# Two of three slices' denominators summed on DVE from a PSUM bank, softmax pieces on POOL, first block first

## The chip, the cores and the metric

The kernel runs on one core of a Trainium2 chip. The core has five engines that run side by side and meet at semaphores: TensorE (PE, matrix products), VectorE (DVE), ScalarE (ACT), GpSimd (POOL) and SyncE (SP, which here issues transfers). The working memory is SBUF. PE writes its results to PSUM, eight banks of 512 float32 columns on 128 partitions; DVE and ACT reach PSUM, POOL has no operand there. The metric is the device time of one execution in microseconds, lower is better. Before the change it is 1321.46 us, the median of three runs (1316.26, 1321.46 and 1323.95).

## The reference

Three layers follow each other on 8192 tokens of width D = 192.

```
w   = softmax(weight_gen)                 # per token: 8 heads x 7 taps
out[s, head] = sum_k w[s, head, k] * x[s - 6 + k, head's 24 columns]

h = out @ w_in                            # 192 -> 2048
g = (a0 + a1 h + a2 h^2 + a3 h^3) / (1 + |b0||h| + |b1| h^2 + 1e-6)
x = g @ w_out                             # 2048 -> 192

h = x @ w2_in                             # 192 -> 2048
y = (h * clip(h + 3, 0, 6) / 6) @ w2_out  # 2048 -> 192
```

The four weight matrices arrive as 64-bit floats, which the kernel takes apart into float32 on the chip.

## The kernel before

**Blocks and slices.** The tokens are cut into 17 blocks (`BL`): two of 256 tokens and fifteen of 512. The hidden width 2048 of a block is worked in slices of 512 PSUM columns: 8 slices for a small block (two groups of 128 hidden units beside each other), 16 for a large one, 256 slices in all. A product is split into high and low parts, so `in1`, `out1` (first layer) and `in2` (second layer) are each five matmuls per group of 128 hidden units. `out2` is done in float32, 32 matmuls of 192 columns for every 256 tokens. A pair of 128 tokens (index `u`) is transposed on PE (`xT`) after the convolution.

**The convolution.** A chunk of four tokens per partition (`c`) is loaded by `load_gen` and `load_chunk`; DVE does the softmax in `softmax_a` (maximum, subtraction) and `softmax_b` (sum, reciprocal, multiplication), ACT the exponential between them. `conv_mul` multiplies, on POOL nearly always, and `conv_sum` adds the seven taps on DVE.

**The rational function.** For a slice the numerator is made by `act_l`, `dve_t`, `dve_t2` and the quotient by `act_ln`, `act_exp`, `dve_hi` (high part), `pool_m`, `dve_d`, `pool_lo` (low part). The denominator has two forms. The usual one is `act_u` (|h|), `act_w` (|b1||h| + |b0|), `pool_q` (their product, on POOL), and later `act_q`. In a slice for which `whole(sl)` holds it is `act_v` (|b0 h|, written to SBUF, line 301), `act_s` (|b1| h^2, line 306) and `dve_q`, one `scalar_tensor_tensor` on DVE that adds both and 1 (line 311, both tensor inputs in SBUF). Here `whole` holds for every third of the first 96 slices (`QN`, `QK`, `QS`), 32 slices.

**What sets the order.** `plan()` is a list scheduler that runs before the program is built. Every step is entered with an engine, an assumed cost, a due time (from the constants `T`, `C1`, `XTP`, ...), what it follows and what it takes. At each turn it emits the step that can start first. It fixes one order per engine; on the chip each engine works through its own order and waits where an operand is late. Of PSUM's eight banks two hold `y1` (the first layer's output, one buffer); the other six go to two classes: `h` (first layer's hidden slices, `NH` = 4 at most) and `s` (`xT`, `in2`, `out2`, weight decoding; `NS` at most). At the end of a block `y1` is read out by a chain of five steps on ACT and DVE, `mid_y` to `tail_lo` (line 252); only then can `out1` of the next block start.

**Fill.** Where the plan leaves PE idle before the second layer of block 1, `idle_mm` (line 392) puts products of the identity matrix into the order.

Of the kernel before, what the change touches and what calls it, by code (L numbers as in the profile page):

```python
# [19 lines left out]
def kernel(  # L20
# [115 lines left out]
    def softmax_b(c):  # L136
        g = ex.pop(c)
        sg = two.tile([P, CT * H], F32, tag="mx", name="sg")
        nc.vector.tensor_reduce(out=sg, in_=g, axis=AX.X, op=ALU.add)
        nc.vector.reciprocal(out=sg, in_=sg)  # L140
        w = two.tile([P, K, CT * H], F32, tag="wk", name="wk")
        nc.vector.tensor_tensor(
            out=w.rearrange("p k t -> p t k"),
            in0=g[:, :, :K],
            in1=sg[:, :, None].to_broadcast([P, CT * H, K]),
            op=ALU.mult,
        )
# [5 lines left out]
    NS = 2  # L153
# [145 lines left out]
    def act_v(sl):  # L299
        u = two.tile([P, GW], F32, tag="u", name="u", bufs=NB["u"])  # L300
# [169 lines left out]
    def job_load(j):  # L470
        if moe_w_in.dtype == F32:
            if "w" not in j:
                j["w"] = two.tile(j["shape"], F32, tag="big", name="wf", bufs=ST)
# [10 lines left out]
        load_rows(sv, j["src"])  # L484
# [114 lines left out]
    JPU = 2.426
    PEN = 1.789  # L600
    CP = 2.57
    KP = 0.04
    WIN = 39.62
# [5 lines left out]
    XQ = -4.798
    XTP = 2.356  # L610
    XH = -5.949
    O1 = 4.624
    UM = 1.409
    I2 = -0.923
    SPR = 0.905
    R2 = -0.798
    O2 = 4.117
    OS = 0.714
    EV = 9.672
# [45 lines left out]
    for u, (b, v) in enumerate(UB):  # L665
        t0 = S0[b] * T - (BV[b] - 1 - v) * 8 * T
        c = u // 2
        if u % 2 == 0:
            t = t0 - CV * T
            add("gen", "SP", 0.6, t - XQ * T if c else X0P, load_gen, c, lat=2.0,  # L670
                take=[("wg", 2, [("softmax_b", c)])])
            add("load", "SP", 3.7, t - XQ * T + 1.0 if c else X0P + 0.5, load_chunk, c, lat=2.0,
                take=[("x", 2, [("conv_mul", 2 * c + 1, 1, 1)])])
# [4 lines left out]
        for i in range(2):
            for z in range(2):
# [256 lines left out]
```

## Time and profile before

| | before |
|---|---|
| median of the runs | 1321.46 us |
| the profiled execution | 1323.68 us, of which the span 1321.9 us |
| PE busy | 1293.3 us (98%), 6690 matmuls |
| DVE, ACT, POOL busy | 1117.8, 1134.5, 1149.9 us (85, 86, 87%) |
| mean granted PE clock | 0.992 of full |

The profiled execution is the one that all durations below come from. An engine's orders are in its own time: a long operation on DVE holds up everything that stands behind it in DVE's order. Matmul records overlap (a new one starts before the last has ended), so what a matmul takes from PE is read from one start to the next. A float32 matmul leaves two records; the fill products and `out2` are float32.

### The profile page before, as it was taken

What the parts mean: (1) busy time and instruction counts of PE and PEld (TensorE: products, weight loads), DVE (VectorE), ACT (ScalarE), POOL (GpSimd) and SP (SyncE); (2) the same over time, 40 slices, a digit from 0 to 9 for tenths busy, and PEclk for the clock granted to TensorE, in tenths of its full rate; (3) what the DMA queues carried; (4) which work ended last, traced back from release to release, by engine and by line L of the source; (5) the groups of instructions that cost most, each with busy time, mean ns of one, the idle gap of its engine ahead of it and who ended that gap; (6) DMA issues with size and microseconds to landing.
All of it is one profiled execution on the core that took longest, in us unless ns stands there. A gap on an engine that the chain in (4) does not pass through costs nothing.

```text
span 1321.9 us, 19246 instructions
## 1 busy us (share of the span) xinstructions
PE 1293.3 (98%) x6690; PEld 1136.3 (86%) x6690; DVE 1117.8 (85%) x1664; ACT 1134.5 (86%) x2032; POOL 1149.9 (87%) x921
## 2 busy tenths in 40 slices
PE   9789998999999999999999999999999999999998
PEld 9788886888988889898888889888888988888898
DVE  7989998999999898888899797988979788786841
ACT  6899898889898798989989798998989899897941
POOL 7898998898989889998999999898999989887830
PEclk9989998999999999999999999999999999999999
DMA  7431010101010101001010101001010000000000
GB/s 234 133 120 35 7 35 6 34 13 34 7 44 7 36 4 46 1 7 36 11 40 0 46 1 36 11 7 36 1 42 1 7 7 7 7 1 12 1 13 12
DMA packets 16121, 37.66 MB, mean 28 GB/s; under 512 B 1948, under 2 KB 12314, under 8 KB 16024
## 3 DMA queue, kind: packets, MB, share of 16 engines
q1 hardware_dynamic: 16024, 36.44, 8.5%
q8 instruction: 52, 0.85, 0.3%
q14 instruction: 45, 0.37, 0.1%
HBM read 30.14 MB, written 6.29 MB: 28 GB/s over the span
## 4 chain that ended last, share of the span: by engine, by line
PE 32%; ACT 21%; POOL 20%; DVE 17%; issue 7%; DMA 1%; SPq 0%; POOLq 0%; ACTq 0%; DVEq 0%
PE h L269 15%; PE y L444 10%; POOL w L368 6%; POOL w L331 6%; POOL glo L379 5%; ACT r L346 3%; ACT l L324 3%; DVE ghi L360 3%; ACT w L355 3%; ACT r L351 3%; DVE l L335 3%; POOL prod L167 3%; DVE w L372 2%; ACT w L317 2%; ACT g L427 2%
## 5 line engine op out<-in xcount | busy, mean ns | idle before, releaser
L379 POOL TENSOR_TENSOR glo<-w,r 128x512 fp32r<-128x512 f32 x256 | 334.0, 1306 | 40.6 <-DVE w L372 31.8
L368 POOL TENSOR_TENSOR w<-w,ghi 128x512 f32<-128x512 f32 x256 | 339.0, 1325 | 29.1 <-DVE ghi L360 22.0
L444 PE MATMUL y<-wo,g 128*128 128x192 f32 x2048 | 352.2, 326 | 0.0
L444 PEld LDWEIGHTS y<-wo,g 128*128 128x128 f32 x2048 | 338.6, 190 | 9.7 <-DVE w L372 0.4
L331 POOL TENSOR_TENSOR w<-w,u 128x512 f32<-128x512 f32 x224 | 291.3, 1303 | 26.9 <-ACT w L317 17.5
L372 DVE SCALAR_TENSOR_TENSOR w<-h,acol,w 128x512 f32<-128x512 f32 x256 | 190.8, 746 | 63.5 <-POOL w L368 62.4
L346 ACT ACTIVATE r<-w 128x512 f32<-128x512 f32 x256 | 162.5, 635 | 70.9 <-POOL w L331 57.3
L167 POOL TENSOR_TENSOR prod<-x,wk 128x672 f32<-128x672 f32 x127 | 192.2, 1525 | 16.4 <-DVE xc L182 10.0
L269 PE MATMUL h<-xh,wst 128*128 128x512 f32 (+1 forms) x544 | 206.0, 379 | 0.0
L269 PE MATMUL h<-xl,wst 128*128 128x512 f32 (+1 forms) x544 | 205.7, 378 | 0.0
L324 ACT ACTIVATE l<-h,acol 128x512 f32<-128x512 f32 x256 | 200.4, 783 | 4.3 <-DVE h L339 3.6
L335 DVE TENSOR_TENSOR l<-h,l 128x512 f32<-128x512 f32 x256 | 174.3, 684 | 35.0 <-ACT l L324 32.9
L360 DVE SCALAR_TENSOR_TENSOR ghi<-h,acol,r 128x512 fp32r<-128x512 f32 x256 | 190.1, 743 | 12.4 <-ACT r L351 11.9
L431 DVE SCALAR_TENSOR_TENSOR g<-g,h 128x512 f32<-128x512 f32 x256 | 174.1, 680 | 29.2 <-ACT g L427 28.5
L317 ACT ACTIVATE w<-u,bab 128x512 f32<-128x512 f32 x224 | 183.5, 819 | 14.7 <-POOL glo L379 14.0
L339 DVE SCALAR_TENSOR_TENSOR h<-l,acol,h 128x512 f32<-128x512 f32 x256 | 191.2, 750 | 4.5 <-ACT u L296 1.0
L427 ACT ACTIVATE g<-h 128x512 f32<-128x512 f32 x256 | 153.9, 601 | 13.8 <-PE h L269 13.7
L351 ACT ACTIVATE r<-r 128x512 f32<-128x512 f32 x256 | 161.6, 632 | 2.7
L355 ACT ACTIVATE w<-w 128x512 f32<-128x512 f32 x224 | 140.4, 627 | 0.0
L296 ACT ACTIVATE u<-h 128x512 f32<-128x512 f32 x224 | 132.8, 593 | 2.0 <-PE h L269 2.0
L408 PE MATMUL y<-ghi,wo1h 128*128 128x512 f32 (+1 forms) x272 | 114.3, 420 | 7.1 <-DVE xl L252 7.0
L269 PEld LDWEIGHTS h<-xl,wst 128*128 128x128 f32 x544 | 103.0, 189 | 19.3
(80 smaller groups left out, 2390.9 us busy)
## 6 DMA issues: line engine op xcount, KB each, us to landing
x<-in_x_dram SPq DMA_DIRECT2D x14, 960.0 KB, 4.7
st<-in_moe_w_out_dram SPq DMA_DIRECT2D x16, 384.0 KB, 3.2
out_dram<-osb SPq DMA_DIRECT2D x32, 192.0 KB, 1.8
st<-in_moe_w_in_dram SPq DMA_DIRECT2D x8, 512.0 KB, 4.9
st<-in_moe_w_in_dram SPq DMA_DIRECT2D x8, 256.0 KB, 4.4
wg<-in_weight_gen_dram SPq DMA_DIRECT2D x16, 112.0 KB, 2.9
x<-in_x_dram SPq DMA_DIRECT2D x1, 768.0 KB, 12.0
x<-in_x_dram SPq DMA_DIRECT2D x2, 216.0 KB, 4.8
```

The lines of the kernel that those rows point to most:

```text
L167: eng.tensor_tensor(out=pr.rearrange("p (h g) k -> p k h g", g=G), in0=xch[c][:, t : t + K, hs].rearrange("p k (h g) -> p k h g", g=G), in ...
L269: nc.tensor.matmul(out=dst, lhsT=l[:, fs], rhs=r, start=(n == 0), stop=(n == len(seq) - 1), skip_group_check=True,)
L317: nc.scalar.activation(out=w, in_=e1[sl]["u"], func=AF.Identity, scale=bab[:, 1:2], bias=bab[:, 0:1])
L324: nc.scalar.activation(out=l, in_=h1[sl], func=AF.Identity, scale=acol[:, 3:4], bias=acol[:, 2:3])
L331: nc.gpsimd.tensor_tensor(out=e["w"], in0=e["w"], in1=e["u"], op=ALU.mult)
L335: nc.vector.tensor_tensor(out=e["l"], in0=h, in1=e["l"], op=ALU.mult)
L346: nc.scalar.activation(out=r, in_=e["w"], func=AF.Ln, bias=0.0 if whole(sl) else CEPS)
L360: nc.vector.scalar_tensor_tensor(out=ghi, in0=h, scalar=acol[:, 0:1], in1=e["r"], op0=ALU.add, op1=ALU.mult)
L368: nc.gpsimd.tensor_tensor(out=m, in0=m, in1=g1[sl][0].bitcast(F32), op=ALU.mult)
L372: nc.vector.scalar_tensor_tensor(out=m, in0=h1.pop(sl), scalar=acol[:, 0:1], in1=m, op0=ALU.add, op1=ALU.subtract)
L379: nc.gpsimd.tensor_tensor(out=glo, in0=e["m"], in1=e["r"], op=ALU.mult)
L444: nc.tensor.matmul(out=y2[b, v][:, s, :], lhsT=g2[b, q][:, c : c + P], rhs=wo2[:, n, :], start=(n == 0 and s == 0), stop=(n == NF - 1), sk ...
```

## The change

The sum of the denominator reads |b0 h| from a PSUM bank, which `act_v` now writes; the bank is of class `s`, whose limit goes from 2 to 3. `whole` holds for two of every three slices, over the whole run: 171 instead of 32. The subtraction and the multiplication of the softmax become steps of their own, which the planner gives to POOL or DVE (POOL for 14 of 16 and 15 of 16 chunks). `conv_mul` no longer follows the `conv_mul` before it. The rows of the first chunk that block 0 does not need are loaded last, and the first two weight loads are issued by ACT instead of SP. The planner's constants are other numbers.

```diff
+        cut_at = ROWS - 2 if c == 0 else ROWS
+        segs = [(0, P, neg, cut_at)]
...
+        if cut_at < ROWS:
+            segs.append((0, P, cut_at, ROWS))
...
+    def softmax_d(c, e):
         g = wgt[c]
+        (nc.vector if e == "DVE" else nc.gpsimd).tensor_tensor(
+            out=g, in0=g, in1=mxs.pop(c)[:, :, None].to_broadcast([P, CT * H, K]),
+            op=ALU.subtract,
         )
...
+    def softmax_m(c, e):
         w = two.tile([P, K, CT * H], F32, tag="wk", name="wk")
-        nc.vector.tensor_tensor(
+        (nc.vector if e == "DVE" else nc.gpsimd).tensor_tensor(
...
-    NS = 2
+    NS = 3
...
     def act_v(sl):
-        u = two.tile([P, GW], F32, tag="u", name="u", bufs=NB["u"])
+        u = bank(("act_v", sl), [P, GW], "v")
...
-            job_load(j)
+            job_load(j, nc.scalar if key in order[:2] else nc.sync)
...
-    QN = 96
+    QN = 256
     QK = 3
-    QS = [0]
+    QS = [0, 1]
...
-    LP = -21.519
+    LP = 2.713
...
+            soft = (("POOL", 0.55, 0.0), ("DVE", 1.0, PEN))
+            add("softmax_a", "DVE", 0.34, t - SM * T, softmax_a, c, after=[("gen", c)])
+            add("softmax_d", soft, 0, t - SM * T + 0.5, softmax_d, c, after=[("softmax_a", c)])
...
-                    after=[("load", c), ("softmax_b", c)] + [("conv_mul",) + k for k in prev],
+                    after=[("load", c), ("softmax_m", c)],
...
             add("act_v", "ACT", 0.57, t + 1.1 - C1, act_v, sl, after=[("in1", sl), ("bab",)],
-                take=[("u", NB["u"], [("dve_q", sl)])])
+                take=[("s", NS, [("dve_q", sl)])])
...
-            add("dve_q", "DVE", 1.0, t + 2.3 - C1, dve_q, sl, after=[("act_v", sl), ("act_s", sl)])
+            add("dve_q", "DVE", 0.661, t + 2.3 - C1, dve_q, sl, after=[("act_v", sl), ("act_s", sl)])
```

The plan moves instructions on every engine. Three places follow; an `x` and a number behind a row is a repeat.

DVE before, at the softmax of the second chunk (`wg`, `mx`, `ex`, `sg`, `wk` are its tiles) and the first denominator sum (`w<-w,u`):

```order
L128 TENSOR_REDUCE mx<-wg 128x32
L129 TENSOR_TENSOR wg<-wg,mx 128x224
L507 SCALAR_TENSOR_TENSOR dt<-dt,st 128x512
L139 TENSOR_REDUCE sg<-ex 128x32
L140 RECIPROCAL sg<-sg 128x32
L142 TENSOR_TENSOR wk<-ex,sg 128x32x7
L311 SCALAR_TENSOR_TENSOR w<-w,u 128x512
L335 TENSOR_TENSOR l<-h_271,l 128x512
```

And DVE after, at the softmax of the same chunk:

```order
L132 TENSOR_REDUCE mx<-wg 128x32
L349 SCALAR_TENSOR_TENSOR h_297<-l,acol,h_297 128x512
L382 SCALAR_TENSOR_TENSOR w<-h_274,acol,w 128x512
L517 SCALAR_TENSOR_TENSOR dt<-dt,st 128x384
L146 TENSOR_REDUCE sg<-ex 128x32
L147 RECIPROCAL sg<-sg 128x32
```

The subtraction and the multiplication have left DVE, and this softmax now comes behind work of block 0.

PE before, at the transposes (`xT`) of block 1's tokens; `L392` are fill products, `L408` to `L412` are `out1` of block 0's fourth slice:

```order
L408 MATMUL y_180<-ghi,wo1h 128x256
L409 MATMUL y_180<-ghi,wo1l 128x256
L410 MATMUL y_180<-ghi,wo1s 128x256
L411 MATMUL y_180<-glo,wo1h 128x256
L412 MATMUL y_180<-glo,wo1s 128x256
L392 MATMUL y_180<-ident 128x128 x8
L197 MATMUL xT<-ident,xc 128x128
L198 MATMUL xT<-ident,xc 128x128
```

PE after, at the same transposes; the `out1` ahead of them is that of block 0's first slice:

```order
L418 MATMUL y_168<-ghi,wo1h 128x256
L419 MATMUL y_168<-ghi,wo1l 128x256
L420 MATMUL y_168<-ghi,wo1s 128x256
L421 MATMUL y_168<-glo,wo1h 128x256
L422 MATMUL y_168<-glo,wo1s 128x256
L402 MATMUL y_168<-ident 128x128 x9
L207 MATMUL xT<-ident,xc 128x128
L208 MATMUL xT<-ident,xc 128x128
```

Block 1's transposes move ahead of three slices of block 0's `out1`. In all the order holds 192 fill products instead of 217.

PE before, between the last `out1` of block 2 (into `y_1616`) and the first of block 3 (into `y_2320`):

```order
L412 MATMUL y_1616<-glo,wo1s 128x512
L269 MATMUL h_2297<-xh_1749,win0hi 128x512
L269 MATMUL h_2297<-xl_1750,win0hi 128x512
L269 MATMUL h_2297<-xh_1749,wst_82 128x512
L269 MATMUL h_2297<-xl_1750,wst_82 128x512
L269 MATMUL h_2297<-xh_1749,win0lo 128x512
L408 MATMUL y_2320<-ghi,wo1h 128x512
```

And PE after, between the same two:

```order
L422 MATMUL y_1621<-glo,wo1s 128x512
L279 MATMUL h_2267<-xh_1695,win0hi 128x512
L279 MATMUL h_2267<-xl_1696,win0hi 128x512
L279 MATMUL h_2267<-xh_1695,wst_82 128x512
L279 MATMUL h_2267<-xl_1696,wst_82 128x512
L279 MATMUL h_2267<-xh_1695,win0lo 128x512
L279 MATMUL h_2290<-xh_1695,win0hi 128x512
L279 MATMUL h_2290<-xl_1696,win0hi 128x512
L279 MATMUL h_2290<-xh_1695,wst_82 128x512
L279 MATMUL h_2290<-xl_1696,wst_82 128x512
L279 MATMUL h_2290<-xh_1695,win0lo 128x512
L418 MATMUL y_2301<-ghi,wo1h 128x512
```

Two `in1` slices instead of one now stand in the gap.

## Rows read from the trace of the kernel before

**Rows 1.** Busy time by stretch: each engine's busy us (instructions), clock, DMA.

```profile
0.00:288.00 288.00, 264.60 (x1627) 240.55 (x1627) 262.54 (x398) 249.44 (x457) 259.56 (x220) 0.96 0.23 70
288.00:596.00 308.00, 306.85 (x1503) 265.82 (x1504) 282.53 (x418) 269.93 (x482) 278.29 (x219) 1.00 0.06 21
596.00:1208.00 612.00, 611.36 (x3001) 531.40 (x3000) 514.80 (x764) 549.68 (x980) 562.55 (x445) 1.00 0.05 16
```

**Rows 2.** Timeline of PE in a late block: start, us, what.

```profile
849.35 0.39 PE L409 MATMUL y<-ghi,wo1l 128*128 128x512 f32 x1
849.58 0.39 PE L410 MATMUL y<-ghi,wo1s 128*128 128x512 f32 x1
```

**Rows 3.** The critical chain, stretch 325 to 340: start, us, what.

```profile
332.62 2.60 PE y L444 x16
```

**Rows 4.** Groups by line, PE: busy us, mean ns of one, idle before.

```profile
L269 PE MATMUL h<-xh,wst 128*128 128x512 f32 x480 | 187.4, 390 | 0.0
L392 PE MATMUL y<-ident 128*128 128x128 f32 x434 | 57.9, 292 | 1.4 <-POOL ident masks.py:199 1.4
```

**Rows 5.** What PE waited for in 0 to 290 us: total, times, longest.

```profile
PE xT L198 <- ACT xc L191: 7.9, 3, 4.8
PE y L408 <- DVE xl L252: 7.0, 3, 4.8
PE h L269 <- DVE w L372: 2.6, 2, 2.3
```

**Rows 6.** Timeline of PE at block 1's transposes.

```profile
58.15 0.27 PE L197 MATMUL xT<-ident,xc 128*128 128x128 f32 x1
63.26 0.47 PE L198 MATMUL xT<-ident,xc 128*128 128x128 f32 x1 [4.84 <-ACT xc L191]
```

**Rows 7.** Timeline of DVE there.

```profile
57.31 4.79 DVE L311 SCALAR_TENSOR_TENSOR w<-w,u 128x512 f32<-128x512 f32 x1
```

**Rows 8.** Timeline of ACT there.

```profile
62.14 0.63 ACT L346 ACTIVATE r<-w 128x512 f32<-128x512 f32 x1 [3.80 <-DVE w L311]
```

**Rows 9.** Timeline of POOL there.

```profile
60.30 1.25 POOL L331 TENSOR_TENSOR w<-w,u 128x512 f32<-128x512 f32 x1
```

**Rows 10.** Timeline of PE at the turn from block 2 to block 3.

```profile
203.85 0.39 PE L269 MATMUL h<-xh,win0lo 128*128 128x512 f32 x1
209.06 0.80 PE L408 MATMUL y<-ghi,wo1h 128*128 128x512 f32 x1 [4.82 <-DVE xl L252]
```

**Rows 11.** Line 311 alone: shortest, median and longest ns, first and last start.

```profile
L311 DVE SCALAR_TENSOR_TENSOR w<-w,u x32: 673/1052/4793, 25.0 to 485.3; 128x512 f32<-128x512 f32 x32
```

**Rows 12.** Groups by line on DVE.

```profile
L372 DVE SCALAR_TENSOR_TENSOR w<-h,acol,w 128x512 f32<-128x512 f32 x256 | 190.8, 746 | 63.5 <-POOL w L368 62.4
L311 DVE SCALAR_TENSOR_TENSOR w<-w,u 128x512 f32<-128x512 f32 x32 | 39.9, 1245 | 1.8 <-ACT w L306 1.4
L129 DVE TENSOR_TENSOR wg<-wg,mx 128x224 f32<-128x224 f32 x16 | 18.3, 1146 | 0.6
L142 DVE TENSOR_TENSOR wk<-ex,sg 128x224 f32<-128x224 f32 x16 | 15.2, 948 | 0.6
```

**Rows 13.** Groups by line on ACT and POOL.

```profile
L317 ACT ACTIVATE w<-u,bab 128x512 f32<-128x512 f32 x224 | 183.5, 819 | 14.7 <-POOL glo L379 14.0
L355 ACT ACTIVATE w<-w 128x512 f32<-128x512 f32 x224 | 140.4, 627 | 0.0
L296 ACT ACTIVATE u<-h 128x512 f32<-128x512 f32 x224 | 132.8, 593 | 2.0 <-PE h L269 2.0
L306 ACT ACTIVATE w<-h,root 128x512 f32<-128x512 f32 x32 | 21.9, 686 | 0.8 <-DVE l L335 0.4 <-POOL glo L379 0.2
L301 ACT ACTIVATE u<-h,bab 128x512 f32<-128x512 f32 x32 | 21.8, 680 | 0.5 <-PE h L269 0.5
L331 POOL TENSOR_TENSOR w<-w,u 128x512 f32<-128x512 f32 x224 | 291.3, 1303 | 26.9 <-ACT w L317 17.5 <-DVE l L335 9.3
L167 POOL TENSOR_TENSOR prod<-x,wk 128x672 f32<-128x672 f32 x127 | 192.2, 1525 | 16.4 <-DVE xc L182 10.0 <-DMA x<-in_x_dram 4.7 <-issue 1.4
```

More of the change, by code (lines that the diff above doesn't have):

```diff
@@ L123, in load_chunk @@
         xch[c] = t
+    mxs = {}
     def softmax_a(c):
+        mxs[c] = two.tile([P, CT * H], F32, tag="mx", name="mx")
+        nc.vector.tensor_reduce(out=mxs[c], in_=wgt[c], axis=AX.X, op=ALU.max)
+    def softmax_d(c, e):
         g = wgt[c]
-        mx = two.tile([P, CT * H], F32, tag="mx", name="mx")
-        nc.vector.tensor_reduce(out=mx, in_=g, axis=AX.X, op=ALU.max)
-        nc.vector.tensor_tensor(
-            out=g, in0=g, in1=mx[:, :, None].to_broadcast([P, CT * H, K]), op=ALU.subtract
+        (nc.vector if e == "DVE" else nc.gpsimd).tensor_tensor(
+            out=g, in0=g, in1=mxs.pop(c)[:, :, None].to_broadcast([P, CT * H, K]),
+            op=ALU.subtract,
         )
@@ L136, in softmax_b @@
     def softmax_b(c):
-        g = ex.pop(c)
         sg = two.tile([P, CT * H], F32, tag="mx", name="sg")
-        nc.vector.tensor_reduce(out=sg, in_=g, axis=AX.X, op=ALU.add)
+        nc.vector.tensor_reduce(out=sg, in_=ex[c], axis=AX.X, op=ALU.add)
         nc.vector.reciprocal(out=sg, in_=sg)
+        mxs[c] = sg
+    def softmax_m(c, e):
         w = two.tile([P, K, CT * H], F32, tag="wk", name="wk")
-        nc.vector.tensor_tensor(
+        (nc.vector if e == "DVE" else nc.gpsimd).tensor_tensor(
             out=w.rearrange("p k t -> p t k"),
-            in0=g[:, :, :K],
-            in1=sg[:, :, None].to_broadcast([P, CT * H, K]),
+            in0=ex.pop(c)[:, :, :K],
+            in1=mxs.pop(c)[:, :, None].to_broadcast([P, CT * H, K]),
             op=ALU.mult,
@@ L459, with load_rows @@
     ST = 8
-    def load_rows(dst, src):
+    def load_rows(dst, src, eng):
         srcs = src if isinstance(src, list) else [src]
@@ L464, in load_rows, with job_load @@
         for i, a in enumerate(srcs):
-            nc.sync.dma_start(out=dst[i * n : (i + 1) * n], in_=a)
+            eng.dma_start(out=dst[i * n : (i + 1) * n], in_=a)
     def flat(t):
         return t if len(t.shape) == 2 else t.rearrange("p f d -> p (f d)")
-    def job_load(j):
+    def job_load(j, eng):
         if moe_w_in.dtype == F32:
@@ L483, in job_load @@
             sv = sv.rearrange("p (f d) -> p f d", f=shape[1])
-        load_rows(sv, j["src"])
+        load_rows(sv, j["src"], eng)
         j["st"] = st
@@ L595 @@
     X0P = -112.0
-    LP = -21.519
+    LP = 2.713
     JP0 = 7.655
     JPT = 2.744
[L599 to L603, printed above, removed]
+    JPU = 2.458
+    PEN = 2.351
+    CP = 0.946
+    KP = 0.118
+    WIN = 41.47
     SWL = 14.0
     BETA = 0.009
-    C1 = -12.512
-    CV = 3.049
+    C1 = -13.219
+    CV = 3.155
     SM = 5.662
[L609 to L619, printed above, removed]
+    XQ = -11.533
+    XTP = 2.81
+    XH = -3.719
+    O1 = 4.488
+    UM = 4.195
+    I2 = -0.894
+    SPR = 0.852
+    R2 = -0.625
+    O2 = 4.833
+    OS = 0.939
+    EV = 10.467
     IDLE = 0.2
@@ L670 @@
             add("gen", "SP", 0.6, t - XQ * T if c else X0P, load_gen, c, lat=2.0,
-                take=[("wg", 2, [("softmax_b", c)])])
+                take=[("wg", 2, [("softmax_m", c)])])
             add("load", "SP", 3.7, t - XQ * T + 1.0 if c else X0P + 0.5, load_chunk, c, lat=2.0,
                 take=[("x", 2, [("conv_mul", 2 * c + 1, 1, 1)])])
-            add("softmax_a", "DVE", 1.7, t - SM * T, softmax_a, c, after=[("gen", c)])
-            add("softmax_e", "ACT", 0.28, t - SM * T + 2.0, softmax_e, c, after=[("softmax_a", c)])
-            add("softmax_b", "DVE", 2.0, t - SM * T + 4.0, softmax_b, c, after=[("softmax_e", c)],
+            soft = (("POOL", 0.55, 0.0), ("DVE", 1.0, PEN))
+            add("softmax_a", "DVE", 0.34, t - SM * T, softmax_a, c, after=[("gen", c)])
+            add("softmax_d", soft, 0, t - SM * T + 0.5, softmax_d, c, after=[("softmax_a", c)])
+            add("softmax_e", "ACT", 0.28, t - SM * T + 2.0, softmax_e, c, after=[("softmax_d", c)])
+            add("softmax_b", "DVE", 0.7, t - SM * T + 3.0, softmax_b, c, after=[("softmax_e", c)])
+            add("softmax_m", soft, 0, t - SM * T + 4.0, softmax_m, c, after=[("softmax_b", c)],
                 take=[("wk", 2, [("conv_mul", 2 * c + 1, 1, 1)])])
```

3 lines of the change are left out of this document (1 added, 2 removed).

## The prediction

> **What bounds the kernel now.** I read busy time by stretch first [rows 1]. PE is busy 264.6 of the first 288 us, 306.85 of the next 308 and 611.36 of the 612 after that. A busy PE may still stall, since records overlap, so I looked at the distance from one start to the next: 0.23 us for a 512-column matmul, with nothing between [rows 2], and 2.60 us for 16 records of `out2`, 0.1625 each [rows 3]. With these the matmuls that compute can be priced. There are 3600 of 512 columns (the row of 480 shown is two of the operand forms [rows 4]; all forms together are 2400 in L269 and 1200 in `out1`), 3600 x 0.2265 = 815 us; 480 of 256 columns at half, 54 us; 2048 records of `out2`, 333 us; the transposes some 14 us. That is 1216 us, which this change leaves as it is. The span is 1321.9, so at most 106 us can be won.
>
> Where do they lie? Up to the first `out1` of block 4, which starts at about 288 us, PE's order holds 198 us of computing matmuls (counted with the same prices). So 90 us are lost before 288 us and some 16 in the 1034 us after it, the last output among them. The late blocks are as fast as PE allows; what the change can win lies in the ramp. There the engines behind PE are all full: DVE 262.5 of 288 us (91%), POOL 90%, ACT 87% [rows 1], because the weights are decoded in the same time. PE's own losses in the ramp are 57.9 us of fill [rows 4], and waits: 7.9 us for the transposes' operand, 7.0 for the read-out of `y1`, 2.6 for a bank that `dve_d` frees [rows 5].
>
> One of these waits shows what the change touches. PE stood 4.84 us between two transposes of block 1, waiting for ACT's copy [rows 6]. ACT had waited 3.80 us in its order on a denominator sum [rows 8]. That sum, both of whose tensor inputs lie in SBUF, lasted 4.79 us on DVE [rows 7], and ended half a microsecond after the last of a row of POOL operations, at 61.55 [rows 9]. The same line takes 0.673 us at its shortest, 1.052 in the median [rows 11]. A `scalar_tensor_tensor` of the same size with one input in PSUM takes 0.746 us [rows 12], in 256 cases.
>
> **The change part by part.** *The denominator's sum.* Its duration with |b0 h| in PSUM is not in the trace. From below, 0.673 us, the shortest of the old form [rows 11]; from above 1.245, its mean [rows 12]. I take 0.746, from line 372, which has the same shape and one input in each memory. *`act_v` into PSUM*: between 0.593 (line 296) and 0.686 (line 306) [rows 13]; I take 0.66. *Softmax pieces on POOL*: 224 columns; by line 331 224/512 x 1.303 = 0.57, by line 167 224/672 x 1.525 = 0.51 [rows 13], and not over 1.303; I take 0.6.
>
> *The two forms of a slice.* Changing one from the usual form to the other takes 1.303 from POOL, takes 0.593 + 0.819 + 0.627 from ACT and gives it 0.66 + 0.686, so -0.69, and gives DVE 0.746.
>
> *The ramp, by DVE's order.* Up to the first gate product of the second layer in block 3 (about 294 us before) DVE's order loses 5 of 6 softmax subtractions (-5.7 us at 1.146) and 4 of 5 multiplications (-3.8 at 0.948); it has 36 denominator sums instead of 18: 36 x 0.746 - 18 x 1.245 = +4.4 [rows 12]. On balance three other operations are gone, -2.2 at line 372's 0.746. Sum -7.3 us. ACT, by the same mark, has 18 slices of the other form more, -12 us, and POOL -23 with +5 for its softmax pieces. DVE is the fullest, and at 91% busy its time is -7.3 / 0.91 = -8.0 us.
>
> *The ramp, by PE's order.* 25 fill products less; a fill product (two records) covers 57.9 / 217 = 0.267 us [rows 4], so -6.7 us. The stall of 4.84 us [rows 6] goes with its cause. At the turn to block 3 PE stood from 203.85 to 209.06, with one `in1` to cover the read-out [rows 10]; a second covers 5 x 0.2265 = 1.1 us more. Sum -12.6. The two sums measure one ramp from two sides. I take -11, nearer to PE's, since PE sets the end.
>
> *The first block.* Its loads and products stand earlier: the first chunk's last two rows come last, the first two weights are issued by ACT, and block 1's transposes move ahead of three `out1`. Past this, chunk 1's loads now stand behind twelve weight loads on SP, instead of five. Only eight weight buffers exist, so SP waits there for the fourth weight to be split on POOL. Chunk 1 belongs to block 2, whose first `in1` starts near 118 us, so I cost this at nothing; the cover is the 60 us between. ACT's three issues are hidden in its 38.6 us of idle time in the ramp [rows 1].
>
> *The late blocks.* From 596 to 1208 us eight blocks pass, 76.5 us each, DVE busy 64.4 of them [rows 1]. Per block the change adds 16 x 2/3 sums x 0.746 = 8.0 us to DVE and takes 2.1 (one softmax), so 70.3 of 76.5, 92%. That is where DVE stands from 288 to 596 us, 91.7%, and there PE is busy 99.6% instead of 99.9%. The difference over some 700 us is +2 us. POOL falls from 70.3 to 57 us per block and ACT from 68.7 to 61, which makes both easier; so between 0 and +4, I take +2. From 288 to 596 DVE stays about level, so nothing.
>
> *Sum.* -11 + 2 = -9 us. The profiled execution took 1323.68 us, 2.2 above the median of the runs, so it becomes 1314.7, and on the median's scale 1312.5. I say 1312.
>
> **The rivals.** *A, the ramp does not follow.* If latency sets the ramp (load, decode, split, first product) then less work on DVE only makes its waits longer, and the late +2 eats the rest. For it: fill is planned idle time and the order still has 192 of 217 products. Against it: three engines at 87 to 91% in the ramp. The fold's 1.1 us and part of the fill remain: -2 us, 1319.5.
>
> *B, the ramp gains much more.* The 4.79 us sum is the worst of 32; a waiting sum holds every step behind it on DVE, and ACT and PE in turn. If what PE waits for in the ramp goes altogether (7.9 + 7.0 + 2.6 [rows 5]) on top of the fill's 6.7, it is -24 and with the late blocks -22: 1299.5. Against it: the read-out of `y1` is a chain of its own, which the denominator does not touch.
>
> *C, slower: banks.* `h` may hold four and `s` three of six banks, so seven claims for six. The |b0 h| of 171 slices is held from `act_v` to `dve_q`; a PE step whose bank is late stops PE, behind which all products stand. The rows have this wait already: PE for `dve_d`, 2.6 us in 2 times, 1.3 us each [rows 5]. If one in eight of the 171 slices has such a wait, it is 21 x 1.3 = +28 us, and with the ramp's -11 and the late +2, +19: 1340.5. It decides from 7 waits on, one slice in 24, where the 9 us are used up. Against it: the usual form keeps its `h` bank through POOL's product and three more steps on ACT, so a bank of `h` now comes free earlier.
> The Trainium skill speaks for C (ScalarE: Activation LUTs, the hint on ScalarE writing to PSUM): such a write has the lower latency, but pays only if TensorE doesn't need most of PSUM. Here PE's products use all eight banks, so by that rule the bank costs more than it saves; no row here shows a write from PSUM to PSUM.
>
> *D, the change does not do what it says*: the sum is no faster with an input in PSUM. Then the ramp's DVE sum is -7.3 + 36 x 0.5 = +11 us, and a late block asks 75.6 of 76.5 us from DVE, which no stretch of the trace reached (its best is 91.7%); at 92% a block takes 82 us, and 9 blocks 50 us: 1380. Against it: 256 rows of line 372 from 0.746.
>
> *E, POOL is the bound, not PE.* POOL's late share is 92%, the highest beside PE. If it set the blocks' time, 57 us instead of 70.3 would leave DVE as the next, at the least 70.3 us a block, 6.2 less than now: nine blocks and the ramp's -11 make -67, 1254.5. Against it: in such a block matmuls start 0.23 us apart without a gap [rows 2], and 76.5 us is what the prices above give for one block (240 x 0.2265 + 128 x 0.1625 and the transposes, 76).
> The Trainium skill speaks for E (Perfetto Trace Analysis, Identifying the Most-Contended Engine): PE is to be judged by its LDWEIGHTS busy time, not by matmul time. By this, 531.4 of 612 us or 87% [rows 1], a late block would have 10 us in reserve; the trace does not agree, by the same starts.
>
> **How the numbers follow.** The forecast 0.46 (1306 to 1318), A 0.21 (1317 to 1323), B 0.17 (below 1306), C 0.12, D 0.03, E 0.01. A measurement of this kernel tells about 0.5% from no change, 6.6 us, so faster is below 1314.9 and slower above 1328. Faster: B and E whole and 0.40 of the forecast's 0.46, 0.58. Same: A and the forecast's upper end, 0.27. Slower: C and D, 0.15. The range is 1297 to 1328: it leaves out a third of B and E (0.06) and most of C and D (0.13).
>
> **What would show it.** Right: the sum's mean near 0.75 us and its longest below 1 us; DVE's softmax lines at one or two instances; fill of 384 records; no wait over 4 us at block 1's transposes; PE's stall at block 3's turn near 4 us; PE busy at 99.5% or more from 300 us on; first `out1` of block 4 at about 277 us. Wrong in the late blocks: PE waiting for `dve_q` or `dve_d` at L269. Wrong in the ramp: the same start of block 4 as before, with DVE's busy share below 88%. The prediction falls if the late blocks take over 77.5 us each.

## The result and the profile after

The changed kernel takes 1306.08 us, the median of six runs (1305.05 to 1307.87); the kernel before, in six runs, 1321.95 (1316.26 to 1323.95). The ratio is 0.9885, 95% interval 0.9866 to 0.9904. That is 15.9 us faster; 1312 was predicted, 1297 to 1328 as the range. The kernel before has two groups of times (of 53 executions beside the experiments 16 from 1316.5 to 1319.5 us and 37 from 1321.3 to 1324.7, for a reason that is not known); its median and its profile belong to the upper one, and against the lower one each gain over it is some 5 us smaller.

The windows of the changed kernel (stretch, its length, then busy us of PE, PEld, DVE, ACT, POOL with their instructions, clock, DMA share) answer to [rows 1]; its span is 1304.0 us.

```profile
0.00:288.00 288.00, 270.91 (x1643) 243.27 (x1644) 268.52 (x431) 252.10 (x466) 250.85 (x222) 0.98 0.24 74
288.00:596.00 308.00, 306.83 (x1511) 267.46 (x1511) 279.90 (x433) 259.18 (x455) 238.41 (x194) 1.00 0.06 21
596.00:1208.00 612.00, 610.86 (x3009) 533.01 (x3009) 547.84 (x842) 512.93 (x898) 464.70 (x373) 1.00 0.04 15
```

POOL has gone from 92% to 76% of the late stretch, DVE from 84% to 90%, and PE is as full as it was. The denominator's sum, which is line 321 now, answers to [rows 11] (shortest, median and longest ns):

```profile
L321 DVE SCALAR_TENSOR_TENSOR w<-w,v x171: 672/677/690, 22.6 to 1239.1; 128x512 f32<-128x512 f32 x171
```

With an input in PSUM none of 171 sums lasts over 0.690 us; before, half of 32 lasted over 1.052. Groups by line of the changed kernel (busy us, mean ns, idle before), for [rows 4, 12, 13]:

```profile
L382 DVE SCALAR_TENSOR_TENSOR w<-h,acol,w 128x512 f32<-128x512 f32 x256 | 190.2, 744 | 34.1 <-POOL w L378 33.2
L321 DVE SCALAR_TENSOR_TENSOR w<-w,v 128x512 f32<-128x512 f32 x171 | 116.1, 679 | 22.3 <-ACT w L316 21.3
L136 DVE TENSOR_TENSOR wg<-wg,mx 128x224 f32<-128x224 f32 x2 | 0.8, 393 | 0.1
L311 ACT ACTIVATE v<-h,bab 128x512 f32<-128x512 f32 x171 | 112.9, 660 | 21.4 <-PE h L279 18.9 <-PE y L422 0.8 <-DVE w L382 0.7
L152 POOL TENSOR_TENSOR wk<-ex,sg 128x224 f32<-128x224 f32 x15 | 9.3, 617 | 0.7 <-DVE sg L147 0.7
L136 POOL TENSOR_TENSOR wg<-wg,mx 128x224 f32<-128x224 f32 x14 | 8.2, 584 | 0.0
L402 PE MATMUL y<-ident 128*128 128x128 f32 x384 | 47.7, 281 | 1.4 <-POOL ident masks.py:199 1.4
```

PE at block 1's transposes and at the turn from block 2 to block 3 (start, us, what, idle before it), for [rows 6, 10]:

```profile
55.73 0.28 PE L207 MATMUL xT<-ident,xc 128*128 128x128 f32 x1
55.84 0.27 PE L208 MATMUL xT<-ident,xc 128*128 128x128 f32 x1
...
193.40 0.40 PE L279 MATMUL h<-xh,win0lo 128*128 128x512 f32 x1
196.10 0.79 PE L418 MATMUL y<-ghi,wo1h 128*128 128x512 f32 x1 [2.30 <-DVE xl L262]
```

The stall of 4.84 us is gone, that of 4.82 us is 2.30. What PE waited for over the whole run (total, times, longest), for [rows 5], is small change:

```profile
PE h L279 <- DVE w L382: 3.0, 5, 1.2
PE xT L207 <- DVE g L441: 2.5, 5, 0.6
PE xT L208 <- ACT xc L201: 2.4, 2, 1.8
PE y L421 <- POOL glo L389: 2.4, 4, 1.2
PE y L418 <- DVE xl L262: 2.3, 1, 2.3
```

**Where the time went.** From its first matmul to its last, counted from the start of one to that of the next, PE's time falls into three parts (the 5.1 us ahead of the first and behind the last are left out; they are the same in every kernel here). Matmuls that compute take 1218.1 us in every kernel (the prices of [rows 2, 3] alone give 1216.6; with these "all else" below would be 1.5 higher throughout, its differences the same). Fill took 55.4 us and takes 48.6. All else (PE late for an operand, or at a lower clock) was 43.3 us and is 32.2. Together -17.9, which is the difference of the spans. Of it -14.6 lie before 250 us and -3.3 behind.

### The profile page after: what moved, and what is told of

The parts are those of the page before. It is cut to its first block, busy times and chain, and to the rows that moved or that the text cites. A ratio compares the mean times of both kernels' runs of the same rounds, so it can differ in the third digit from the quotient of the medians.

```text
span 1304.0 us, 18918 instructions
## 1 busy us (share of the span) xinstructions
PE 1281.1 (98%) x6640; PEld 1127.2 (86%) x6640; DVE 1143.5 (88%) x1774; ACT 1069.3 (82%) x1893; POOL 984.3 (75%) x811
## 3 DMA queue, kind: packets, MB, share of 16 engines
q10 hardware_dynamic: 304, 1.05, 0.3%
## 4 chain that ended last, share of the span: by engine, by line
PE 85%; ACT 7%; DVE 3%; POOL 2%; DMA 1%; issue 1%; SPq 0%; POOLq 0%; ACTq 0%
PE h L279 41%; PE y L454 24%; PE y L418 4%; PE y L421 4%; PE y L419 4%; PE y L420 4%; PE y L422 4%; ACT r L361 1%; ACT l L334 1%; ACT st L511 1%; ACT ys L230 1%; ACT r L356 1%; ACT w L316 1%; PE xT L207 1%; ACT v L311 1%
## 5 line engine op out<-in xcount | busy, mean ns | idle before, releaser
L378 POOL TENSOR_TENSOR w<-w,ghi 128x512 f32<-128x512 f32 x256 | 330.9, 1295 | 44.1 <-DVE ghi L370 32.0
L177 POOL TENSOR_TENSOR prod<-x,wk 128x672 f32<-128x672 f32 x127 | 189.4, 1503 | 17.3 <-DVE xc L192 12.1
L356 ACT ACTIVATE r<-w 128x512 f32<-128x512 f32 x256 | 161.2, 634 | 19.4 <-DVE w L321 15.3
L321 DVE SCALAR_TENSOR_TENSOR w<-w,v 128x512 f32<-128x512 f32 x171 | 116.1, 679 | 22.3 <-ACT w L316 21.3
L311 ACT ACTIVATE v<-h,bab 128x512 f32<-128x512 f32 x171 | 112.9, 660 | 21.4 <-PE h L279 18.9
L316 ACT ACTIVATE w<-h,root 128x512 f32<-128x512 f32 x171 | 117.9, 690 | 7.8 <-DVE l L345 6.5
L279 PEld LDWEIGHTS h<-xh,wst 128*128 128x128 f32 x544 | 103.1, 189 | 20.8 <-POOL wst L532 1.5
L341 POOL TENSOR_TENSOR w<-w,u 128x512 f32<-128x512 f32 x85 | 109.8, 1292 | 12.3 <-ACT w L327 10.6
```

The costliest lines, as they stand in the source:

```text
L177: eng.tensor_tensor(out=pr.rearrange("p (h g) k -> p k h g", g=G), in0=xch[c][:, t : t + K, hs].rearrange("p k (h g) -> p k h g", g=G), in ...
L279: nc.tensor.matmul(out=dst, lhsT=l[:, fs], rhs=r, start=(n == 0), stop=(n == len(seq) - 1), skip_group_check=True,)
L356: nc.scalar.activation(out=r, in_=e["w"], func=AF.Ln, bias=0.0 if whole(sl) else CEPS)
L378: nc.gpsimd.tensor_tensor(out=m, in0=m, in1=g1[sl][0].bitcast(F32), op=ALU.mult)
```

## The experiments

The times below are medians of several runs each, beside runs of the kernel before on the same chip (medians 1322.0 to 1322.9). In the table, "block 4" is the start of its first `out1`; "fill" and "other" are PE's two parts as above, in us; "span", "block 4", "fill" and "other" are of the one profiled execution; the rows of before and changed are repeated for comparison. Where the order of PE differs, the starts of block 4 are no fair comparison, and the span decides.

| kernel | us | ratio to before, interval | span | block 4 | fill | other |
|---|---|---|---|---|---|---|
| before | 1322.3 | | 1321.9 | 288.1 | 55.4 | 43.3 |
| changed | 1306.1 | 0.9885 [0.9866, 0.9904] | 1304.0 | 270.7 | 48.6 | 32.2 |
| E1 before, sum from PSUM | 1310.6 | 0.9922 [0.9903, 0.9941] | 1308.6 | 278.0 | 53.7 | 31.8 |
| E2 changed, sum from SBUF | 1348.2 | 1.0205 [1.0183, 1.0227] | 1346.0 | 285.3 | 53.2 | 69.6 |
| E3 softmax on DVE, new plan | 1318.3 | 0.9981 [0.9968, 0.9993] | 1316.0 | 280.0 | 56.1 | 36.6 |
| E4 first loads as before | 1305.5 | 0.9884 [0.9865, 0.9903] | 1303.8 | 270.5 | 48.5 | 32.1 |
| E5 E1, no subtraction | 1308.7 | 0.9911 [0.9891, 0.9931] | 1308.5 | 278.6 | 56.1 | 29.2 |
| E6 E1, fewer products | 1304.6 | 0.9878 [0.9854, 0.9901] | 1302.8 | 274.9 | 54.5 | 25.1 |
| E7 changed, late sum twice | 1344.6 | 1.0183 [1.0158, 1.0208] | 1344.9 | 271.3 | 50.4 | 71.2 |
| E8 fewer whole slices, new plan | 1322.5 | 1.0010 [0.9996, 1.0024] | 1320.1 | 277.3 | 59.0 | 37.9 |
| E9 softmax on DVE, same order | 1310.3 | 0.9911 [0.9897, 0.9925] | 1308.1 | 273.7 | 50.7 | 34.2 |
| E10 changed, POOL loaded | 1332.6 | 1.0083 [1.0066, 1.0100] | 1330.7 | 278.5 | 49.8 | 57.7 |
| E11 changed, old constants | 1309.6 | 0.9906 [0.9892, 0.9920] | 1307.8 | 277.5 | 53.3 | 31.2 |
| E12 changed, half the fill | 1306.1 | 0.9881 [0.9862, 0.9901] | 1304.3 | 271.0 | 41.1 | 39.9 |

**E1 and E2: where the sum reads |b0 h|.** E1 keeps the order of the kernel before and lets its 32 sums read h's PSUM bank. E2 keeps the changed kernel's order and puts |b0 h| back into SBUF, where it shares three buffers with |h|.

```diff
 E1, on the kernel before
-            out=e["w"], in0=e["w"], scalar=CEPS, in1=e["u"], op0=ALU.add, op1=ALU.add
+            out=e["w"], in0=e["w"], scalar=CEPS, in1=h1[sl], op0=ALU.add, op1=ALU.add
 E2, on the changed kernel, in act_u and act_v
-        u = two.tile([P, GW], F32, tag="u", name="u", bufs=NB["u"])
+        u = two.tile([P, GW], F32, tag="u", name="u", bufs=3)
...
-        u = bank(("act_v", sl), [P, GW], "v")
+        u = two.tile([P, GW], F32, tag="u", name="v", bufs=3)
```

> The kernel before with its own order, one operand changed: the 32 denominator sums on DVE read the hidden slice h, which lies in PSUM, in place of |b0 h| in SBUF. So the denominator is computed with h instead of |b0 h|; everything else, the order on every engine included, is as before. Theory (DVE paces the ramp, and a sum with both inputs in SBUF is held up by POOL): the sum falls from a mean of 1.245 us to 0.68 and its longest from 4.79 us to below 0.7; 32 x 0.57 = 18 us less on DVE in the first 490 us, 10 us of it before block 4; the 4.84 us stall at block 1's transposes goes; the time falls by 6 to 10 us, to 1312 to 1316. Rival (the gain comes from the new order and the earlier loads): the sum gets shorter all the same, but the time falls by at most 2 us. Rival (POOL's relief makes the gain): no change, since POOL does the same work.

> The changed kernel with its own order; |b0 h| goes to an SBUF tile (one ring of three with |h|) instead of the PSUM bank, which stays empty. Theory: the sum goes back to 1.1 to 1.25 us, 171 x 0.5 = 85 us more on DVE; a late block asks about 75 of 76.5 us from DVE, which then sets its time; the time rises by 30 to 70 us over the changed kernel, to 1335 to 1375, slower than before. Rival (order and loads): at most 10 us more, 1316. Rival (POOL's relief): about 5 us more, since POOL does as little as in the changed kernel.

E1 took 11.7 us off the kernel before with nothing moved: 13.3 of its span. Its sums, by line (shortest, median, longest):

```profile
L311 DVE SCALAR_TENSOR_TENSOR w<-w,h x32: 667/678/690, 25.0 to 472.1; 128x512 f32<-128x512 f32 x32
```

E2 lost 42 us. Its sums, and who waited for them (us, times):

```profile
L321 DVE SCALAR_TENSOR_TENSOR w<-w,v x171: 673/823/1859, 22.9 to 1281.6; 128x512 f32<-128x512 f32 x171
...
  ACT r L356: 50.8, 66
```

The shortest sum is the same, 0.67 us, wherever the input lies; only the slow ones differ. In E2 the mean is 0.993 us (169.8 us for 171), 54 us more on DVE, and ACT's wait for the sum is 50.8 us instead of 15.3. The three shared buffers cost nothing that is seen: at the two writes ACT waits for PE's products (14.8 us, 25.2 in the changed kernel), not for a buffer. So the time of the old sum was not its own but time held, and the records show by what. In E2, at 881 us, a sum starts while a product on POOL runs and ends 0.54 us after that product's end; POOL's next operation, which starts while the sum still runs, takes 1.73 us instead of 1.3:

```profile
880.72 1.30 POOL L378 TENSOR_TENSOR w<-w,ghi 128x512 f32<-128x512 f32 x1 [0.99 <-DVE ghi L370]
881.98 1.73 POOL L389 TENSOR_TENSOR glo<-w,r 128x512 fp32r<-128x512 f32 x1
```

```profile
881.15 1.41 DVE L321 SCALAR_TENSOR_TENSOR w<-w,v 128x512 f32<-128x512 f32 x1
```

Of the sums that last 0.75 us or more, 19 of 26 in the kernel before and 96 of 113 in E2 end 0.54 to 0.56 us after the end of a POOL operation; with an input in PSUM none of E1's 32 and none of the changed kernel's 171 does. The Trainium skill (SBUF — State Buffer, Who interferes with whom) says that a DVE instruction with two SBUF inputs contends with a GpSimd instruction that reads SBUF, and one with at most one SBUF input, outside its two-port modes, does not. These runs agree: with one input in PSUM 32 of 32 sums in E1 and 171 of 171 in the changed kernel stay at or below 0.690 us.

**E3 and E9: the softmax pieces.** E3 gives all of them to DVE and lets the planner run; E9 keeps every order of the changed kernel but that of POOL and DVE at those 29 pieces.

```diff
 E3
-            soft = (("POOL", 0.55, 0.0), ("DVE", 1.0, PEN))
+            soft = (("DVE", 1.0, 0.0), ("DVE", 1.0, 0.0))
 E9, in both functions
-        (nc.vector if e == "DVE" else nc.gpsimd).tensor_tensor(
+        nc.vector.tensor_tensor(
```

> The changed kernel with the softmax subtraction and multiplication on DVE for all 16 chunks; the planner orders anew with that. Theory: 29 operations of about 1 to 1.2 us come back to DVE, both inputs in SBUF, 8 to 9 us of them before block 4: the ramp loses 4 to 8 us, 1310 to 1314, with late blocks unchanged. Rival (order and loads): within 2 us of the changed kernel's 1306.

> The changed kernel with the order of all its steps kept; only the engine of the softmax pieces is changed, all 32 on DVE. The earlier run with them on DVE took 1318.3 us, but on a new plan with 34 more fill products (34 x 0.224 = 7.6 us), so it could not price the pieces. Theory 1 (DVE's work does not pace the ramp; a run that took 5.7 us of DVE's work off it gained nothing): within 3 us of the changed kernel, 1305 to 1309 us, and the rest of the earlier run's loss was its plan. Theory 2 (the prediction's: work on DVE in the ramp costs the ramp, divided by DVE's share): some 9.5 us of pieces before block 4 cost 9 to 11 us, 1315 to 1317 us.

E3 lost 12.2 us, E9 4.2 (3.0 by block 4, in the same order of PE). What is left of E3, 8 us, is its plan, not the pieces; that plan has 37 fill products more than the changed kernel (458 records), not 34. E9's pieces on DVE (busy us, mean ns):

```profile
L152 DVE TENSOR_TENSOR wk<-ex,sg 128x224 f32<-128x224 f32 x16 | 13.5, 842 | 0.2
...
L136 DVE TENSOR_TENSOR wg<-wg,mx 128x224 f32<-128x224 f32 x16 | 10.0, 625 | 0.1
```

Up to the start of block 4 eight pieces are moved: DVE's ten take 7.0 us where its two took 0.9, so 6.1 us more of DVE's work (and 4.8 less of POOL's), and 3.0 us were lost: work on DVE has a price there, about half its length. Theory 1 put it at nothing, theory 2 at 9 to 11; both missed.

**E4: the first block.** The cut of the first chunk and ACT's weight loads are undone.

```diff
-        cut_at = ROWS - 2 if c == 0 else ROWS
+        cut_at = ROWS
...
-            job_load(j, nc.scalar if key in order[:2] else nc.sync)
+            job_load(j, nc.sync)
```

> The changed kernel with the first chunk loaded in one piece and all weight loads issued by SP, as before; the order of work on every engine is the same. Theory: the first products start 0.3 to 1 us later and this is lost among the waits behind, 1306 to 1308. Rival (the earlier first block makes much of the gain): 4 us or more, 1310 and over.

No difference (1305.5 for 1306.1). The loads of the title are worth nothing that can be measured. The earlier place of block 1's transposes is part of the order and was not taken apart from it.

**E5 and E6: which engine paces the ramp.** Both start from E1. E5 leaves out the softmax's subtraction (16 operations of 1.1 us on DVE), E6 POOL's product in every third slice (85 of 1.3 us).

```diff
 E5
-        nc.vector.tensor_tensor(
-            out=g, in0=g, in1=mx[:, :, None].to_broadcast([P, CT * H, K]), op=ALU.subtract
-        )
 E6
-        nc.gpsimd.tensor_tensor(out=e["w"], in0=e["w"], in1=e["u"], op=ALU.mult)
+        if sl % 3 != 1:
+            nc.gpsimd.tensor_tensor(out=e["w"], in0=e["w"], in1=e["u"], op=ALU.mult)
```

> The kernel before with its own order, its 32 sums reading h from PSUM as in e1, and the softmax subtraction left out: 16 DVE operations with both inputs in SBUF, 1.146 us each, 5 of them ahead of block 4 (the exponential is taken of the weights themselves). Theory (DVE's work in the ramp sets its time): 5.7 us less DVE work ahead of block 4, so 4 to 6 us less than e1, 1305 to 1307. Rival (what e1 won was only the one long sum and its stall): no further gain, 1309 to 1312.

> The kernel before with its own order, its 32 sums reading h from PSUM as in e1, and POOL's product of the denominator left out in every slice of index 1 modulo 3 (85 slices, in which the denominator is |b1||h| + |b0| + 1): the slices in which the changed kernel spares POOL this product. ACT's and DVE's orders are the same. Theory (DVE paces the ramp): POOL's 85 x 1.3 = 111 us less gain at most 2 us, 1308 to 1311. Rival (POOL's relief makes the changed kernel's other 5 us): 1304 to 1307.

E5 gained nothing in the profiled execution (span 1308.5 for 1308.6) and 1.9 us in the median (1308.7 for 1310.6), far less than the theory's 4 to 6; E6 gained 5.8 us of the span (3.1 of it by block 4) and 6.0 in the median. The windows from 60 to 200 us fit this. E1 first, then E6 (columns as above):

```profile
60.00:200.00 140.00, 127.31 (x817) 116.63 (x816) 131.46 (x209) 130.81 (x238) 133.68 (x110) 0.98 0.17 52
```

```profile
60.00:200.00 140.00, 128.69 (x817) 116.99 (x816) 131.92 (x212) 132.02 (x240) 123.00 (x101) 0.98 0.16 50
```

In E1 POOL is the fullest behind PE, 133.7 of 140 us or 95%, and taking work from DVE (94%) changes little. With POOL at 88% the ramp gets shorter. It isn't that POOL holds DVE less: the softmax's 32 operations on DVE, which still have both inputs in SBUF, take 33.5 us in E6 and 33.1 in E1. The kernel before and the changed kernel, in this order:

```profile
60.00:200.00 140.00, 128.77 (x811) 119.13 (x812) 131.81 (x201) 125.75 (x228) 128.05 (x104) 0.95 0.17 54
```

```profile
60.00:200.00 140.00, 131.00 (x802) 118.04 (x801) 135.69 (x219) 129.00 (x237) 127.06 (x108) 0.96 0.15 48
```

Before, DVE was the fullest (131.8, 94%), for its sums were held. In the changed kernel it is again (135.7, 97%), now with work. So E9's pieces cost something there and E5's in E1 little. This reads as if what paces the ramp went from one engine to the next as work is moved; the shares fit that in four kernels but do not show it, and E10 has a case where they mislead.

**E7: DVE in the late blocks.** From slice 128 on the sum is done a second time, into a tile that nobody reads.

```diff
+        if sl >= 128:
+            junk = two.tile([P, GW], F32, tag="junk", name="junk", bufs=1)
+            nc.vector.scalar_tensor_tensor(
+                out=junk, in0=e["w"], scalar=CEPS, in1=e["u"], op0=ALU.add, op1=ALU.add
+            )
```

> The changed kernel with its own order; from slice 128 on (block 9 and later) the denominator's sum is done a second time into an unused tile: 86 DVE operations of 0.68 us more, 7.2 us in a block. DVE then asks about 75.3 of a block's 76.45 us, 98%. Theory of the prediction (near 92% PE already loses, 0.2 us a block): a block grows to 79 to 82 us, 1325 to 1350. Rival (PE loses only when DVE's work exceeds the block, since buffers cover single waits): a block stays below 77 us, 1306 to 1311.

Blocks that took 76.45 us take 81.8 (seven blocks from 651.6 to 1223.9 us): 7.2 us more of DVE's work cost 5.3. Its late window and PE's waits:

```profile
596.00:1208.00 612.00, 589.41 (x2823) 500.00 (x2822) 567.85 (x876) 487.34 (x850) 444.23 (x356) 0.99 0.04 14
```

```profile
PE xT L207 <- DVE g L446: 7.5, 10, 1.3
PE h L279 <- DVE w L387: 7.1, 11, 1.2
PE h L279 <- DVE junk L326: 6.9, 9, 1.5
PE y L423 <- DVE xl L262: 6.8, 8, 2.3
```

In the seven blocks alone DVE is busy 526.5 of 572.3 us, 92%. So DVE has no 7 us to spare in a late block of the changed kernel, where it is busy 90%. E7 does not part the share of DVE from the place of the added work: each second sum holds up what stands behind it, and it also keeps the bank of |b0 h| longer, for which PE waits 6.9 us in 9 times, of the 40.9 us that the span grew.

**E8: fewer slices of the new form.** `whole` as before (every third of the first 96), all else as changed, planned anew.

```diff
-    QN = 256
+    QN = 96
-    QS = [0, 1]
+    QS = [0]
```

> The changed kernel with the denominator summed on DVE in every third of the first 96 slices, as before (32 sums, from PSUM), the rest of the change as it is; the planner orders anew. Theory (DVE paces the ramp): DVE has 18 sums, 12 us, less ahead of block 4 than the changed kernel, so the ramp is no slower, 1302 to 1308. Rival (POOL's and ACT's relief pays): POOL's 18 products, 23 us, come back ahead of block 4, and the late blocks have POOL at 92% again: 1312 to 1318.

It lost the whole gain: 1322.5 us, 12 slower than E1, which has the same 32 slices. Its plan holds 456 fill records where the changed kernel has 384, and late blocks take 77.2 us with PE waiting for `dve_d` 17 times (9.1 us). So the constants seem to fit one set of steps, and E3 and E8 price plan and step together. What the 139 further slices of the new form are worth by themselves, in one and the same order, was not tried and stays open.

**E10: POOL loaded.** A product that nobody reads is put on POOL in every third slice, 85 in all.

```diff
+        if sl % 3 == 1:
+            junk = two.tile([P, 4, P], F32, tag="junk", name="junk", bufs=1)
+            four = ident[:, None, :].to_broadcast([P, 4, P])
+            nc.gpsimd.tensor_tensor(out=junk, in0=four, in1=four, op=ALU.mult)
```

> The changed kernel with a product that nothing needs added on POOL in every third slice, 85 of some 1.3 us: it takes away the relief that the change gave POOL, and nothing else. Theory 1 (POOL's relief is the second part of the gain): 5 to 8 us are lost, 1311 to 1314 us, about 3 of them by block 4 and the rest in the late blocks, with POOL near 92% before block 4. Theory 2 (the second part is the order, with fewer fill products): no change, 1305 to 1307 us. Theory 3 (POOL's operations slow DVE's whenever they run): the sums with one operand in PSUM grow over 0.75 us in the mean and the loss is over 10 us.

It lost 26.5 us, four times what theory 1 gave, and the sums stay at 0.680 us, so theory 3 isn't the reason. Its late window, and DVE's wait for POOL:

```profile
596.00:1208.00 612.00, 603.09 (x2944) 520.31 (x2943) 540.04 (x829) 503.31 (x880) 499.15 (x411) 1.00 0.04 15
```

```profile
L386 DVE SCALAR_TENSOR_TENSOR w<-h,acol,w 128x512 f32<-128x512 f32 x256 | 190.8, 746 | 62.5 <-POOL w L382 61.3
```

POOL is busy 82% of this stretch, and blocks take 78.1 us; in E1 it is busy 92%, and they take 76.6 (PE is busy 611.34 of 612). The share doesn't decide. 1.04 us that the plan doesn't know hold up the product behind it, and DVE's step `dve_d` waits 61 us for POOL instead of 33. So E10 shows that POOL's place in the chain is dear, not what the change's relief of POOL is worth; E6 alone bears on that, in the old order.

**E11 and E12: the order, and the fill.** E11 has the changed code with all the planner's constants of the kernel before (`LP`, `JPU`, `PEN`, `C1` and so on). E12 keeps the changed order and halves the fill.

```diff
 E11 (and 18 more such lines)
-    LP = 2.713
+    LP = -21.519
 E12
-        for i in range(n):
+        for i in range(n if first else n // 2):
```

> The changed kernel's steps, planned with the priorities of the kernel before: the code's change alone, without its new table of numbers. The plan has 207 fill products where the changed kernel has 192, 15 x 0.224 = 3.4 us of PE. If PE's work sets the time, 1309 to 1311 us. If the order that the new numbers make were the gain (the prediction's second sum of 12.6 us for the ramp), 1316 us or more, near the run with nothing but the sums from PSUM (1310.6) or above it. If the numbers don't matter, 1305 to 1307 us.

> The changed kernel in its own order, with half of the fill products in every place but the first: 117 instead of 192, 75 fewer, which filled 75 x 0.25 = 19 us of PE. Nothing else is left out. Theory 1 (fill is cover: PE would wait there for the engines behind it in any case): PE stands idle instead, its waits in the ramp grow by about 19 us, and the time stays within 3 us of the changed kernel, 1303 to 1309 us. Theory 2 (fill is a cost: it runs longer than the wait it stands in, as 18 fill products more in the run with the old constants would have it, which lost 3.5 us): 75 x 0.19 = 14 us gained, some 1292 us. Theory 3 (the idle time takes PE's granted clock down, as it stood at 0.96 before and 0.98 after in the first 288 us): the clock there falls below 0.95 and the time is 1312 us or more.

E11 lost 3.5 us (it holds 420 fill records, 210 products, three more than expected). E12 lost nothing with 75 fill products less. Its window of the ramp and its fill:

```profile
0.00:288.00 288.00, 260.46 (x1492) 231.85 (x1493) 268.18 (x430) 251.71 (x465) 250.31 (x222) 0.96 0.24 73
```

```profile
L402 PE MATMUL y<-ident 128*128 128x128 f32 x234 | 33.0, 296 | 1.4 <-POOL ident masks.py:199 1.4
```

PE's fill fell by 7.5 us and its other loss rose by 7.7: each product that is left takes longer (41.1 / 117 = 0.35 us from start to start, 48.6 / 192 = 0.25 before), at a granted clock of 0.96 for 0.98 in the mean, and PE's waits grew. Every start from block 1 on is within 0.4 us of the changed kernel's. Fill is cover here. So E11's 3.5 us are not likely the price of its fill; that its order brings the engines behind PE later, and that the fill only shows it, is argued and not shown.

## Why the prediction was right, and where its steps failed

**The chain of the gain.** Three kernels lie on one way: the sum from PSUM alone (E1), 1322.3 to 1310.6, -11.7 us; the rest of the code with the old constants (E11), to 1309.6, -1.0; the new constants, to 1306.1, -3.5. The first step is shown with nothing else moved, the third with nothing but the constants. The second is no more than the spread of the runs, and what it holds (139 more slices on DVE, POOL's relief, the softmax pieces) was not taken apart in one order. The forecast of 1312 was 6 us too high, at the very edge of the 1306 to 1318 that it gave itself: the ramp gave 3.6 us more than forecast and the late blocks 5.3, while the medians moved 2.0 less than the profiled spans.

**The sum.** 0.746 us was taken between bounds of 0.673 and 1.245; it is 0.679, at the lower end. The nearest row was not used. Line 431 has the same operation and shape, one input in PSUM, and takes its scalar as a number, as the sum does; line 372 reads its scalar from a tile (`acol`):

```profile
L431 DVE SCALAR_TENSOR_TENSOR g<-g,h 128x512 f32<-128x512 f32 x256 | 174.1, 680 | 29.2 <-ACT g L427 28.5
```

`act_v` (0.660 for 0.66) and the pieces on POOL (0.584 and 0.617 for 0.6) came as taken.

**The ramp, -11, measured -14.6 up to 250 us.** The sum by DVE's order becomes, with 36 x 0.679, -9.7 us, / 0.91 = -10.7. E1 shows the bulk of it: 18 of its sums lie in the ramp, 24.6 us before (1.367 each, more than the 1.245 of all 32) and 12.2 in E1, and block 4 starts 10.1 earlier. So 12.4 us of DVE's time gave 10.1 of the ramp's; the division by DVE's share, which would give 13.6, had the wrong direction. As a rule it fails further: E5 takes six subtractions ahead of block 4 from DVE, 5.6 us in E1, and gains 1.9 us at most. The term for the subtractions, -5.7, was not to be had from E1's state. Nor do they take 1.146 us each there: ahead of block 4 their mean is 0.997 in the kernel before. That -11 came within 3.6 us of the ramp's -14.6 is in part luck.

**The ramp by PE's order.** The stall of 4.84 us went with its cause, as said, and it goes in E1 too, with the sum alone (0.72 us are left of it there). The turn to block 3 was to keep near 4 us and is at 2.30; block 4 was to start at about 277 us and starts at 270.7. The fill's term, 25 x 0.267 = -6.7, is the size of what was seen (-6.8) but no cause: E12 takes away three times as many products and the time stays. Counting fill as a saving counts the ramp's gain a second time; that the two sums came out near each other was not the check that it seemed.

**The first block at nothing.** Right: E4.

**The late blocks, +2, measured -3.3.** The sign was wrong. The price came from the stretch of 288 to 596 us, where PE was busy 306.85 of 308 [rows 1], put down to DVE's share of 92%. E1 has DVE at 90% there and PE at 308.00 of 308:

```profile
288.00:596.00 308.00, 308.00 (x1518) 268.83 (x1517) 277.67 (x420) 272.37 (x485) 274.37 (x219) 1.00 0.07 24
```

In the old order the loss went with the held sums, whose last ran at 485 us [rows 11]; DVE's share fell with them, so the two are not parted. The changed kernel has no held sum, DVE at 91%, and PE at 306.83 of 308 again. With the shorter sums DVE's late share became 90% and not 92; in E7, at 92 to 93%, a block grows by 5.3 us. The named waits of PE behind 250 us did rise, from 1.0 to 2.5 us, while a late block went from 76.69 to 76.45. What shortened the block by the quarter of a microsecond is not settled. One candidate is POOL's relief: E6, which has it in the old order, takes 76.30 us for every block from block 4 on (PE busy 612.00 of 612 from 596 us), where E1 takes 76.3 to 76.8; the changed kernel takes 76.25 for two of three blocks and 77.0 for the third.

**The rivals.** A (1319.5) and C (1340.5) did not come: the ramp followed, and PE's wait for a bank at line 279 is 3.0 us in 5 times. The Trainium skill's caveat for C (ScalarE: Activation LUTs, the hint on ScalarE writing to PSUM) did not decide here; the write itself takes 0.660 us into PSUM and 0.680 into SBUF [rows 13], so its direction agrees. B's price (1299.5) was 6.6 us too low, about as far off as the forecast: PE's waits shrank, but most of what PE lost ahead of block 4 is left: 77 of 92 us (270.7 less 193.6 of computing matmuls at the prediction's prices, 288.1 less 195.7 before, where the prediction counted 198). D's mechanism is E2's: with held sums the change costs 26 us against the kernel before. D's price for a block at 92% of DVE, 82 us, is what E7 measured, 81.8 at 92%. But 91.7% is not the most that DVE reaches: it is at 94% from 60 to 200 us before and at 97% there in the changed kernel. E fell: POOL went to 76% and the late block stayed.

## What to carry to other kernels

Before adding up work on an engine, look at the spread of one operation: where the shortest is 0.67 us and the median 1.05, as here, the difference can be held time, and moving one operand was worth 11.7 us, the new constants of the plan 3.5. Look also for the row that matches an operation in its scalar, not only in its shape and memories. Fill that a plan puts into PE's order was cover here, not a cost (E12); count it or the engines behind it, not both. Before taking work off an engine, ask whether it is the fullest in that stretch, and ask again after each step; the share is a hint (E5, E6), and the place in the chain can outweigh it (E10).

## What the runs showed of the chip

One operation has many durations: a 128x512 sum on DVE with both inputs in SBUF took 0.67 us at the shortest, 0.99 in the mean in E2, and 4.79 at the worst before, beside POOL's operations of 1.3 us. POOL's are held in turn: in E2 its product at line 378 takes 1.388 us in the mean, in the changed kernel 1.295. The softmax's subtraction of 224 columns on DVE shows the same spread: 1.146 us before [rows 12], 0.625 in E9, 0.393 in the two that the changed kernel leaves there. The two engines' shares of busy time thus hold waiting, which no view of waits names. And PE's granted clock was lower where PE did less: in the first 60 us it is 1.00 of 2.4 GHz in the changed kernel, with PE busy for 52.1 us, and 0.94 in the mean in E12, with PE busy for 46.1. The end did not move (1306.1 us both), and from block 1 on every block starts within 0.4 us of the changed kernel's.
